# A transformer block on one core: a second score tile in some cycles goes to VectorE, and the opening of the attention loop is rearranged

## The chip, the core and the metric

One core of a Trainium2 chip. TensorE does the matmuls, ScalarE (ACT) the exponentials, VectorE (DVE) everything elementwise and a part of the exponentials, GpSimd (POOL) sets memory, and the queue of SyncE (SP) issues most of the DMAs. The metric is the device time of one execution in microseconds; it was measured three times before the change.

## What is computed

```python
h   = x + attention(layernorm(x)) @ wo      # S = 2048, D = 512, 32 heads of 16
out = h + (sigmoid(g) * u) @ w_down         # g, u = layernorm(h) @ w_gate, w_up; F = 1792
```

The attention is plain softmax over all 2048 keys. With 32 heads it needs 32 x 2048 x 2048 exponentials, which is most of the work of the kernel: the heads are so thin (16) that the matmuls around them are short.

## The kernel before, in words

**Prologue** (to 35.9 us). x is loaded, normalised and transposed into `xnT`; K and Q of the first block of eight heads and the first V tiles are computed; and a bound for the softmax is put in a spare row of `QB`, so that no maximum has to be taken later. The last thing before the loop is that bound: `q_bound` (L187) on VectorE writes `bnd`, and `emit_q_bound` (L216) sends two DMAs from it into `QB[0]`, one for heads 0 and 1 of the group, one for heads 2 and 3.

**Main loop** (35.9 to 936 us). The unit is a score tile: 128 keys by 512 queries of one head. Units run over query chunk `qc` (4), group of four heads `g` (8), key tile `kt` (16) and head `j` (4): 2048 units, in **steps** of three (`GU`), 683 steps in all. In a step, `emit_scores` (L669) has TensorE write three banks of `pss` (two such buffers, taken in turn) and ScalarE turn them into bf16 weights `pt` by one ACTIVATE over 1536 columns (L691). `emit_pv` (L739) multiplies four tiles at a time by V into `acc`. Four steps make a **cycle** (`CYC`): twelve units.

Three things set the pace of a cycle:

- In a *split* step the ACTIVATE takes two of the three tiles. The third goes to VectorE, which computes the exponential by bit operations and a polynomial, in five instructions: `exp_bits` in the step itself (L703; it reads `pss`), two of `exp_first` a step later (L706, L709), `exp_second` two steps later (L712) and `exp_third` three steps later (L716). From step `G0` = 28 on, the first step of each cycle is split, save for three in each of chunks 1 to 3, just after the chunk before has ended: 154 steps.
- *Pairs*: the keys of heads 0, 1 and of heads 2, 3 lie in different halves of the rows of the array. From step 28 on every second step uses matmuls of 64 rows (`tile_position`), so that two of different halves can run side by side; the others use all 128 rows.
- *PV batches*: from step 28 on the twelve PV matmuls of a cycle are issued together in the third step of the next cycle; before that, four at a time (`plan_pv`, L799).

**Fill.** Between the scores, `emit_fill` (L759) hands out other matmuls, so many to a step (`rate`, L664): the remaining V tiles, K and Q of the later heads (`fill_v`, `fill_k`, `fill_q0`), Q of the later chunks (`fill_q`), then for each finished chunk the output projection, the second layer norm and the gated feed-forward layer (`ffn_tasks`). All of these share **one** PSUM bank, `pm`: a fill task that needs it waits until VectorE (or ScalarE for the gate's tanh, L496) has read the previous one. A task yields `("gap", n)` where it wants n further steps of rest before the next. What is computed must be ready when a later step asks for it, and the instructions of each engine run in the order in which they were issued; this order is written out by hand (`manual_schedule`), so a wait on any engine holds all that is issued after it there.

**Normalisation.** After the last key tile of a head group, `emit_norm` (L719) copies `acc`, sends the four rows of sums through DRAM into a `[32, 64]` tile, takes reciprocals on VectorE five steps later (L730), sends them back as rows broadcast over partitions, and multiplies ten steps later into `OT` (L736). This happens 31 times.

**Tail** (936 to 991 us). The feed-forward layer of the last chunk, which can't start before the last head is done.

Of the kernel before, what the change touches and what calls it, by code (L numbers as in the profile page):

```python
# [9 lines left out]
FP32 = mybir.dt.float32  # L10
# [7 lines left out]
def kernel(  # L18
# [11 lines left out]
    nc = tc.nc  # L30
    P = 128
# [8 lines left out]
    QC = 512  # L40
    TQ = QC // P
    NQC = S // QC
    GU = 3
    CYC = 4
    RATES = ((2.0, 2.0, 0.0, 3.0), (2.0, 2.5, 0.0, 3.0))
    G0 = 28
    GM = 188
    G1 = 680
    QS = DH ** -0.5 * 1.4426950408889634 * 2.0 ** 23
# [9 lines left out]
    norm = ctx.enter_context(tc.tile_pool(name="norm", bufs=1))  # L59
# [18 lines left out]
    for part in (1, 0, 2):  # L78
        nc.scalar.dma_start(out=wqkv_sb[:, :, part * D:(part + 1) * D],
                            in_=wqkv_v[:, :, part * D:(part + 1) * D])  # L80
# [132 lines left out]
            nc.sync.dma_start(out=QB[n % 2][32 * j:32 * j + 32:2, j, :],  # L213
                              in_=QTu[r:r + DH, g // 2, qc * QC:(qc + 1) * QC])

    def emit_q_bound(n):  # L216
        qc, g = qgs[n]
        assert ("b", qc, g // 2) in ready
        r = 32 * qc + 4 * g
        for h in range(2):  # L220
            nc.sync.dma_start(out=QB[n % 2][64 * h + 1:64 * h + 2, 2 * h:2 * h + 2, :],
                              in_=bnd[r + 2 * h:r + 2 * h + 2, :])

    NV0 = 6
# [1 line left out]
    def prologue(pro):  # L226
# [137 lines left out]
        k_bound()  # L364
        q_bound(0, False)
        ready.add(("b", 0, 0))
        emit_q_bound(0)
        k_spread(ku, 1, slice(0, S), nc.sync)
        gate = pro.tile([32, 1], BF16, name="gate")
        nc.gpsimd.tensor_copy(out=gate[:], in_=bnd[0:32, 0:1])  # L370
# [5 lines left out]
    NS = len(groups)  # L376
    SPC = NS / NQC
# [17 lines left out]
    def fill_k(b):  # L395
        ku = stages[b % 2]
        sqs = []
        for n in range(5):
            if n < 4:
                ps = pm_tile()  # L400
                for c in range(DC):
                    yield 1
                    qk_mm(ps, 1, b, n, c)
                cols = slice(n * QC, (n + 1) * QC)
                nc.vector.tensor_copy(out=ku[:, cols], in_=ps[:])
                sqs.append(squares(ku[:, cols]))
                if n in (0, 2):
                    nc.gpsimd.memset(KT[:, 2 * b + n // 2, :], 1.0)
                yield ("gap", 0)
            if n:  # L410
                pn = pm_tile()
                yield 1
                norm_mm(pn, b, sqs[n - 1][:])
                k_max(pn, b, n - 1)
                yield ("gap", 0)
        for g in (2 * b, 2 * b + 1):
            k_spread(ku, g, slice(0, S), nc.sync)
        k_bound()
        ready.add(("k", b))
# [4 lines left out]
    def fill_q0(b):  # L424
        ps = pm_tile()
        for c in range(DC):
            yield 1
            qk_mm(ps, 0, b, 0, c)
        q_store(QTu[:, b, 0:QC], ps)
        sq = squares(QTu[:, b, 0:QC])  # L430
        yield ("gap", 2)
        pn = pm_tile()
        yield 1
        norm_mm(pn, b, sq[:])
        q_root(pn, 0)
        q_bound(0, True)
        ready.add(("q", 0, b))
        ready.add(("b", 0, b))
        yield ("gap", 0)

    def fill_q(qc):
        cols = slice(qc * QC, (qc + 1) * QC)
        sq4 = stages[qc % 2]
        for b in range(4):
            ps = pm_tile()
            for c in range(DC):
                yield 1
                qk_mm(ps, 0, b, qc, c)
            q_store(QTu[:, b, cols], ps)
            nc.vector.tensor_tensor(out=sq4[:, b * QC:(b + 1) * QC], in0=QTu[:, b, cols], in1=QTu[:, b, cols],  # L450
                                    op=ALU.mult)
            ready.add(("q", qc, b))
            yield ("gap", 3)
        yield ("gap", 2)
        pn = pm_tile()
        for b in range(4):
            yield 1
            norm_mm(pn, b, sq4[:, b * QC:(b + 1) * QC], start=(b == 0), stop=(b == 3))
        q_root(pn, qc)
        q_bound(qc, False)  # L460
        for b in range(4):
            ready.add(("b", qc, b))
        yield ("gap", 0)

    def wo_mm(ps, t, g):
        nc.tensor.matmul(ps[:], lhsT=OT[t // TQ % 2][:, g, t % TQ * P:(t % TQ + 1) * P], rhs=wo_pad[:, g, :],  # L466
# [195 lines left out]
        yield from wo_early(NQC - 1)  # L662

    def rate(i):  # L664
        if i < G0:
            return 4.0 if i < 6 else 2.0
        return (RATES[i >= 3 * SPC][(i - G0) % CYC], 1.0, 1.0, 0.0)[n_pv.get(i, 0)]

    def emit_scores(i):  # L669
        group = groups[i]  # L670
        n = len(group)
        pss = pss2[i % 2]
        pairs = i >= G0 and (i - G0) % 2 == 1
        order = list(enumerate(group))
        if pairs and group[0][3] // 2 == group[1][3] // 2:
            order[1:] = order[:0:-1]
        for ui, (qc, g, kt, j) in order:
            n_qg = qc * NG + g
            assert ("k", g // 2) in ready
            h0 = 64 * (j // 2)  # L680
            rows = slice(h0, h0 + 64) if pairs else slice(0, P)
            nc.tensor.matmul(pss[:, ui, :], lhsT=KT[rows, g, kt * P:(kt + 1) * P],  # L682
                             rhs=QB[n_qg % 2][rows, j, :], start=True, stop=True,
                             tile_position=(h0, 0) if pairs else None)
            if kt == 12 and j == 3 and n_qg + 1 < len(qgs):
                emit_q_rows(n_qg + 1)
                emit_q_bound(n_qg + 1)
        k = (i - G0) % 7 if i >= G0 else i % 4
        pt = pt4[k] if k < 4 else (pt_early if i < GM else pt_late)[k - 4]
        na = n - 1 if i in split else n  # L690
        ex = nc.scalar.activation(out=pt[:, 0:na, :], in_=pss[:, 0:na, :], func=ACT.Exp, scale=DH ** -0.5 / QS)  # L691
        if na < n:
            scratch = early_scratch if i < GM else late_scratch
            tc.declare_no_dep(exp_bits(pss[:, na, :], *scratch).ins, ex.ins,
                              reason="both only read, from different banks")
            later(i + 1, lambda: exp_first(*scratch))
            later(i + 2, lambda: exp_second(*scratch))
            later(i + 3, lambda: exp_third(pt[:, na, :], *scratch))
        for ui, u in enumerate(group):
            p_of[u] = pt[:, ui, :]  # L700

    def exp_bits(src, e_bits, e_man, e_pol):
        return nc.vector.tensor_scalar(out=e_bits, in0=src, scalar1=ONE_BITS, scalar2=0.0, op0=ALU.add, op1=ALU.max)  # L703
# [15 lines left out]
    def emit_norm(qc, g, i):  # L719
        xs = norm.tile([P, QC], FP32, name="xs")  # L720
        nc.vector.tensor_copy(out=xs[:], in_=acc[:])  # L721
        sd = dram.tile([4, QC], FP32, name="sd")
        for j in range(4):
            nc.sync.dma_start(out=sd[j:j + 1, :], in_=xs[32 * j + DH:32 * j + DH + 1, :])
        s32 = norm.tile([32, 64], FP32, name="s32")
        nc.sync.dma_start(out=s32[:], in_=sd[:].rearrange("j (a b) -> (j a) b", b=64))

        def recip():
            r32 = norm.tile([32, 64], FP32, name="r32")
            nc.vector.reciprocal(out=r32[:], in_=s32[:])  # L730
            rd = dram.tile([4, QC], FP32, name="rd")
            nc.sync.dma_start(out=rd[:].rearrange("j (a b) -> (j a) b", b=64), in_=r32[:])
            rb = norm.tile([P, QC], FP32, name="rb")
            for j in range(4):
                nc.sync.dma_start(out=rb[32 * j:32 * j + 32, :], in_=rd[j:j + 1, :].to_broadcast([32, QC]))
            later(i + 10, lambda: nc.vector.tensor_tensor(out=OT[qc % 2][:, g, :], in0=xs[:], in1=rb[:], op=ALU.mult))  # L736
        later(i + 5, recip)
# [52 lines left out]

    LAG = 2

    split = set(range(G0, G1, CYC))
    for qc in range(1, NQC):
        n0 = int(qc * SPC) + 20
        split -= {n for n in range(n0, n0 + 24) if (n - G0) % (2 * CYC) == 0}


    def plan_pv():  # L799
        plan, last = {}, 0  # L800
        for n, group in enumerate(groups):
            if G0 <= n < G1:
                if (n - G0) % CYC == 0:
                    last = n + CYC + 2
                    for k, u in enumerate(units[n * GU:(n + CYC) * GU:4]):
                        if k and u[2] == 0:
                            last += 1
                        plan.setdefault(last, []).append(u)
            else:
                for u in group:  # L810
                    if u[3] == 3:
                        last = max(last, n + LAG)
                        plan.setdefault(last, []).append(u)
        return plan

    with tc.manual_schedule():
# [13 lines left out]
        later(90, lambda: nc.gpsimd.tensor_copy(out=ident_f[:], in_=ident_bf[:]))  # L830
        load_w()
        pv_due = plan_pv()
        n_pv = {i: len(us) if G0 <= i < G1 + CYC else 0 for i, us in pv_due.items()}
        for i in range(NS + LAG):
            if i < NS:
                emit_scores(i)
            for fn in due.pop(i, []):
                fn()
            for u in pv_due.pop(i, []):
                emit_pv(*u[:3], i)  # L840
            if LAG <= i < NS:
                emit_fill(i)
        for _ in fl:
            pass
# [35 lines left out]
```

## Time and profile before

| | |
|---|---|
| median of three runs | 990.5 us (988.42 to 992.69) |
| the profiled execution's own time | 993.14 us, its span 991.4 us |
| main loop in it, first to last exponential | 35.9 to 936.0 us |
| granted TensorE clock, mean | 0.993 |
| an ACTIVATE of 3 tiles / of 2 tiles (128x1536, 128x1024) | 1.49 us / 1.08 us |
| the five VectorE instructions of a split tile | 0.69, 0.42, 0.69, 0.69, 0.68 us |

How to read it: the busy share of an engine (page, part 1) is a mean over a prologue, a long loop and a tail, which have different limits, so the loop is cut into stages by time, and in each stage the question is which engine the next step waited for. ACTIVATEs overlap: one of three tiles lasts 1.49 us, but the next one starts after 1.33 us. The time that counts is that from start to start.

### The profile page before, as it was taken

The numbers are of one execution on the slowest core, as the hardware profiler recorded it, in microseconds if no ns is written. First come the engines' busy times: TensorE is split into PE (matmuls) and PEld (weight loads), VectorE is DVE, ScalarE is ACT, GpSimd is POOL, SyncE is SP. The second block draws the span as 40 slices with busy tenths as digits, with TensorE's granted clock in tenths as the row PEclk, the third lists the DMA queues.
The fourth block names the chain that finished last, engine by engine and source line by source line (L and its number), as shares of the span: only waits on it lengthen the run. The fifth ranks groups of instructions, "written<-read, shape, count | busy, mean of one in ns | idle before, by whom it ended". The sixth has DMA issues, their size and how long they took to land.

```text
span 991.4 us, 14443 instructions
## 1 busy us (share of the span) xinstructions
PE 848.8 (86%) x5197; PEld 282.9 (29%) x5291; DVE 696.1 (70%) x1202; ACT 910.5 (92%) x772; POOL 41.3 (4%) x57
## 2 busy tenths in 40 slices
PE   4898888878788888989888888899888888889998
PEld 2332222222222222223222222223222222223343
DVE  8338898888775776767766777777766776767452
ACT  4799899999999999999999999999999999999731
POOL 4600000000000000000000000000000000000000
PEclk9999999999999999999999999999999999999999
DMA  5002331000003000000000000000100000000100
GB/s 156 20 1 54 101 82 54 15 16 4 20 20 100 15 15 16 14 6 28 26 21 26 16 15 15 15 2 26 32 25 21 15 15 15 14 6 22 45 1 21
DMA packets 26400, 28.06 MB, mean 28 GB/s; under 512 B 8348, under 2 KB 20764, under 8 KB 26328
## 3 DMA queue, kind: packets, MB, share of 16 engines
q1 hardware_dynamic: 24744, 25.56, 9.1%
q10 hardware_dynamic: 1584, 1.57, 0.5%
q8 instruction: 41, 0.67, 0.3%
q14 instruction: 31, 0.25, 0.1%
HBM read 20.18 MB, written 2.61 MB: 23 GB/s over the span
## 4 chain that ended last, share of the span: by engine, by line
PE 49%; ACT 30%; DVE 13%; issue 5%; DMA 1%; POOL 0%; SPq 0%; ACTq 0%; DVEq 0%; POOLq 0%
PE pss L682 24%; ACT pt L691 15%; PE acc L742 9%; ACT stg L691 7%; PE pm L504 5%; ACT QTu L691 4%; PE pm L487 3%; ACT wd L691 3%; PE pm L491 2%; PE pm L466 2%; PE pm L156 2%; ACT sg L496 2%; DVE wd L703 1%; PE pm L151 1%; DVE st L130 1%
## 5 line engine op out<-in xcount | busy, mean ns | idle before, releaser
L682 PE MATMUL pss<-QB,KT 64*128 64x512 bf16 (+1 forms) x2022 | 487.5, 381 | 92.4 <-ACT pt L691 44.3
L691 ACT ACTIVATE pt<-pss 128x1536 bf16<-128x1536 f32 (+1 forms) x404 | 527.3, 1402 | 13.2 <-PE pss L682 12.1
L682 PEld LDWEIGHTS <-KT 128*128 128x128 bf16 (+1 forms) x2048 | 152.4, 95 | 370.0 <-issue 257.4
L691 ACT ACTIVATE stg<-pss 128x1536 bf16<-128x1536 f32 (+1 forms) x140 | 185.9, 1393 | 4.8 <-PE pss L682 4.7
L703 DVE TENSOR_SCALAR stg<-pss 128x512 int32<-128x512 f32 x114 | 78.8, 691 | 129.7 <-PE pss L682 126.2
L742 PE MATMUL acc<-pt,Vaug 128*17 128x512 bf16 x1211 | 115.8, 384 | 2.3 <-DVE xs L721 1.7
L691 ACT ACTIVATE QTu<-pss 128x1024 bf16<-128x1024 f32 (+1 forms) x71 | 98.7, 1390 | 0.4 <-PE pss L682 0.2
L691 ACT ACTIVATE wd<-pss 128x1024 bf16<-128x1024 f32 (+1 forms) x68 | 88.0, 1373 | 2.4 <-PE pss L682 2.0
L709 DVE SCALAR_TENSOR_TENSOR y<-reg 128x512 f32<-128x512 f32 x114 | 79.0, 693 | 3.9
L712 DVE SCALAR_TENSOR_TENSOR y<-y,reg 128x512 f32<-128x512 f32 x114 | 78.6, 690 | 3.3
L487 PE MATMUL pm<-reg,reg 128*128 128x512 bf16 x212 | 62.1, 380 | 10.4 <-DVE reg L500 9.4
L742 PEld LDWEIGHTS <-Vaug 128*17 128x17 bf16 x2048 | 37.8, 89 | 110.3 <-issue 93.6
L491 PE MATMUL pm<-reg,wu 128*128 128x512 bf16 x206 | 62.5, 382 | 1.6 <-issue 1.3
L500 DVE SCALAR_TENSOR_TENSOR reg<-sg,pm 128x512 bf16<-128x512 f32 x56 | 38.3, 683 | 32.1 <-PE pm L491 28.9
L504 PE MATMUL pm<-wd,reg 128*128 128x512 bf16 x211 | 58.8, 381 | 2.0 <-issue 1.3
L742 PE MATMUL acc<-stg,Vaug 128*17 128x512 bf16 x420 | 49.7, 382 | 1.6 <-DVE xs L721 1.6
L706 DVE TENSOR_SCALAR reg<-stg 128x512 int32<-128x512 int32 x114 | 48.4, 424 | 2.8
L496 ACT ACTIVATE sg<-pm 128x512 f32<-128x512 f32 x56 | 35.0, 624 | 16.7 <-PE pm L487 15.6
L156 PE MATMUL pm<-reg 128*128 128x512 bf16 x115 | 35.9, 388 | 7.5 <-DVE y L167 3.7
L703 DVE TENSOR_SCALAR wd<-pss 128x512 int32<-128x512 f32 x40 | 27.5, 688 | 20.7 <-PE pss L682 20.3
L716 DVE SCALAR_TENSOR_TENSOR pt<-y,stg 128x512 bf16<-128x512 f32 x61 | 41.2, 675 | 1.2
L466 PE MATMUL pm<-wo_pad,OT 128*128 128x512 bf16 x117 | 34.9, 382 | 1.0 <-DVE reg L475 0.4
(108 smaller groups left out, 603.2 us busy)
## 6 DMA issues: line engine op xcount, KB each, us to landing
rb<-rd SPq DMA_DIRECT2D x124, 64.0 KB
reg<-in_A_x_dram SPq DMA_DIRECT2D x8, 256.0 KB
QB<-QTu SPq DMA_DIRECT2D x128, 16.0 KB
xr<-in_A_x_dram SPq DMA_DIRECT2D x16, 128.0 KB
out_dram<-ob SPq DMA_DIRECT2D x16, 128.0 KB
sd<-xs SPq DMA_DIRECT2D x124, 2.0 KB
KT<-stg SPq DMA_DIRECT2D x7, 256.0 KB
reg<-in_B_w_gate_dram SPq DMA_DIRECT2D x4, 448.0 KB
```

Of the source, the lines that this page charges most:

```text
L156: nc.tensor.matmul(ps[:], lhsT=wqkv_sb[:, c, w0:w0 + P], rhs=xnT[:, c, n * QC:(n + 1) * QC], start=(c == 0), stop=(c == DC - 1))
L466: nc.tensor.matmul(ps[:], lhsT=OT[t // TQ % 2][:, g, t % TQ * P:(t % TQ + 1) * P], rhs=wo_pad[:, g, :], start=(g == 0), stop=(g == NG - 1))
L487: nc.tensor.matmul(ps[:], lhsT=wg[:, c, f * P:(f + 1) * P], rhs=hnT[:, c, :], start=(c == 0), stop=(c == DC - 1))
L491: nc.tensor.matmul(ps[:], lhsT=wu[:, c, f * P:(f + 1) * P], rhs=hnT[:, c, :], start=(c == 0), stop=(c == DC - 1))
L496: nc.scalar.activation(out=sg[:], in_=ps[:], func=ACT.Tanh, scale=0.5)
L504: nc.tensor.matmul(ps[:], lhsT=hT[:, f, tt * P:(tt + 1) * P], rhs=wd[:, f, :], start=(f == 0), stop=(f == FC - 1))
L682: nc.tensor.matmul(pss[:, ui, :], lhsT=KT[rows, g, kt * P:(kt + 1) * P], rhs=QB[n_qg % 2][rows, j, :], start=True, stop=True, tile_positio ...
L691: ex = nc.scalar.activation(out=pt[:, 0:na, :], in_=pss[:, 0:na, :], func=ACT.Exp, scale=DH ** -0.5 / QS)
L703: return nc.vector.tensor_scalar(out=e_bits, in0=src, scalar1=ONE_BITS, scalar2=0.0, op0=ALU.add, op1=ALU.max)
L709: nc.vector.scalar_tensor_tensor(out=e_pol, in0=m, scalar=PA, in1=m, op0=ALU.add, op1=ALU.mult)
L712: nc.vector.scalar_tensor_tensor(out=e_pol, in0=e_pol, scalar=PB, in1=e_man.bitcast(FP32), op0=ALU.add, op1=ALU.mult)
L742: nc.tensor.matmul(acc[32 * j:32 * j + VW, :], lhsT=Vaug[:, kt, 4 * g + j, :], rhs=p_of.pop((qc, g, kt, j)), start=(kt == 0), stop=(kt == ...
```

## The change

- `split` begins at step 8 instead of 28, and a second split step is added in one of four cycles (`twice`): the third step of cycles that begin at a multiple of 16. That is 29 more, from step 114 to step 658, none of them in the first 45 steps of chunks 1 to 3. Together 188 split steps for 154. The second tile has scratch memory of its own, in the half of `OT` that isn't in use (`scratch_of`).
- PV batches of twelve and the ring of seven `pt` buffers run from step 0, and so does the alternation of pairs. Up to step 44, and in the cycles with two splits, every step uses pairs. 421 steps use them instead of 327.
- `rate`: to step 44, fill of 4, 4 (2 from step 12), 0 and 4 matmuls in the steps of a cycle; 2, 2, 0, 3 in cycles with two splits. Fill starts in step 1 rather than 2. `fill_k` for b > 1, the end of `fill_q0` and the end of `fill_q` each rest one more step.
- The sums are laid out as `[128, 16]` instead of `[32, 64]` for the reciprocal.
- The second of the two first DMAs of the bound is issued from ScalarE's queue instead of SP's.

```diff
-    G0 = 28
+    FIRST = 44
...
-    def emit_q_bound(n):
+    def emit_q_bound(n, engs=(nc.sync, nc.sync)):
...
-            nc.sync.dma_start(out=QB[n % 2][64 * h + 1:64 * h + 2, 2 * h:2 * h + 2, :],
+            engs[h].dma_start(out=QB[n % 2][64 * h + 1:64 * h + 2, 2 * h:2 * h + 2, :],
                               in_=bnd[r + 2 * h:r + 2 * h + 2, :])
...
-        emit_q_bound(0)
+        emit_q_bound(0, (nc.sync, nc.scalar))
...
                     nc.gpsimd.memset(KT[:, 2 * b + n // 2, :], 1.0)
-                yield ("gap", 0)
+                yield ("gap", int(b > 1))
...
                 k_max(pn, b, n - 1)
-                yield ("gap", 0)
+                yield ("gap", int(b > 1))
...
         ready.add(("q", 0, b))
         ready.add(("b", 0, b))
-        yield ("gap", 0)
+        yield ("gap", 1)
...
         for b in range(4):
             ready.add(("b", qc, b))
-        yield ("gap", 0)
+        yield ("gap", 1)
...
     def rate(i):
-        if i < G0:
-            return 4.0 if i < 6 else 2.0
-        return (RATES[i >= 3 * SPC][(i - G0) % CYC], 1.0, 1.0, 0.0)[n_pv.get(i, 0)]
+        if i < FIRST:
+            rates = (4.0, 4.0 if i < 12 else 2.0, 0.0, 4.0)
+        elif i - i % CYC + 2 in twice:
+            rates = (2.0, 2.0, 0.0, 3.0)
+        else:
+            rates = RATES[i >= 3 * SPC]
+        return (rates[i % CYC], 1.0, 1.0, 0.0)[n_pv.get(i, 0)]
...
-        pairs = i >= G0 and (i - G0) % 2 == 1
+        pairs = i % 2 == 1 or i < FIRST or i - i % CYC + 2 in twice
...
-        k = (i - G0) % 7 if i >= G0 else i % 4
+        k = i % 7
...
-            scratch = early_scratch if i < GM else late_scratch
+            scratch = scratch_of(i)
...
+    def scratch_of(i):
+        if i % CYC:
+            flat = OT[(int((i - 20) / SPC) + 1) % 2][:].rearrange("p g q -> p (g q)")
+            return (flat[:, 0:2 * QC].bitcast(mybir.dt.int32), flat[:, 2 * QC:4 * QC].bitcast(mybir.dt.int32),
+                    flat[:, 4 * QC:6 * QC].bitcast(FP32))
+        return early_scratch if i < GM else late_scratch
...
-        s32 = norm.tile([32, 64], FP32, name="s32")
-        nc.sync.dma_start(out=s32[:], in_=sd[:].rearrange("j (a b) -> (j a) b", b=64))
+        s32 = norm.tile([P, 16], FP32, name="s32")
+        nc.sync.dma_start(out=s32[:], in_=sd[:].rearrange("j (a b) -> (j a) b", b=16))
...
-    split = set(range(G0, G1, CYC))
-    for qc in range(1, NQC):
-        n0 = int(qc * SPC) + 20
-        split -= {n for n in range(n0, n0 + 24) if (n - G0) % (2 * CYC) == 0}
+    split = set(range(8, G1, CYC))
+    twice = set()
+    for qc in range(NQC):
+        n0 = int(qc * SPC) + 20
+        if qc:
+            split -= {n for n in range(n0, n0 + 24) if n % (2 * CYC) == 4}
+        lo, hi = (int(qc * SPC) + 45, int((qc + 1) * SPC) + 16) if qc else (112, int(SPC) + 16)
+        twice |= {n + 2 for n in range(lo, min(hi, G1 - 8)) if n % (4 * CYC) == 0}
+    split |= twice
...
-            if G0 <= n < G1:
-                if (n - G0) % CYC == 0:
+            if n < G1:
+                if n % CYC == 0:
...
-            if LAG <= i < NS:
+            if 1 <= i < NS:
                 emit_fill(i)
```

## The prediction, made before the changed kernel ran

> **What bounds the kernel now.** I read the page's busy shares first, since they say which engine to look at:
>
> ```profile
> PE 848.8 (86%) x5197; PEld 282.9 (29%) x5291; DVE 696.1 (70%) x1202; ACT 910.5 (92%) x772; POOL 41.3 (4%) x57
> ```
>
> ScalarE is busy 92% of a span that has a tail and a prologue without exponentials. So the second view is its timeline in the middle of the loop, for the time from start to start:
>
> ```profile
> 568.71 0.60 ACT L496 ACTIVATE sg<-pm 128x512 f32<-128x512 f32 x1
> 569.19 1.04 ACT L691 ACTIVATE stg<-pss 128x1024 bf16<-128x1024 f32 x1
> 570.09 1.49 ACT L691 ACTIVATE QTu<-pss 128x1536 bf16<-128x1536 f32 x1
> 571.42 5.10 ACT L691 ACTIVATE pt<-pss 128x1536 bf16<-128x1536 f32 x4
> 576.37 0.65 ACT L496 ACTIVATE sg<-pm 128x512 f32<-128x512 f32 x1
> ```
>
> Nothing stands between them: three tiles cost 1.33 us, two 0.92 (0.90 here, 0.94 in most cycles), a tanh 0.48. A split tile saves ScalarE 0.41. The loop has 529 ACTIVATEs of three tiles, 154 of two and 42 tanh: 706 + 142 + 20 = 869 us, and lasts 900. The other 31 us are waits of ScalarE. The third view, busy time by stretch (columns: length, then PE, PEld, DVE, ACT, POOL, then the clock), says where they are:
>
> ```profile
> 35.90:83.50 47.60, 44.31 (x239) 15.48 (x242) 18.65 (x34) 44.71 (x33) 12.63 (x9) 1.00 0.05 11
> 83.50:190.60 107.10, 88.39 (x547) 26.92 (x557) 95.07 (x169) 100.81 (x81) 0.00 (x0) 0.98 0.24 65
> 77.60:144.90 67.30, 56.21 (x334) 16.88 (x337) 62.13 (x118) 60.96 (x49) 0.00 (x0) 0.97 0.28 77
> 190.60:291.10 100.50, 81.40 (x519) 25.53 (x526) 79.50 (x134) 99.28 (x81) 1.07 (x2) 0.98 0.06 18
> 291.10:936.00 644.90, 564.07 (x3532) 180.66 (x3594) 453.16 (x746) 635.48 (x534) 9.53 (x22) 1.00 0.07 21
> ```
>
> These are steps 0 to 32, 32 to 112, 28 to 76 (inside the two), 112 to 192, and the rest. By the same count ScalarE needs 42.3, 98.6, 98.6 and 629.5 us in the four that tile the loop, so it waits 5.3, 8.5, 1.9 and 15.4. In the first TensorE is full (93%); in steps 28 to 76 VectorE is (92%), because fill and split tiles meet there. From 291 on ScalarE bounds, with single stalls of this kind (VectorE, TensorE, ScalarE):
>
> ```profile
> 589.70 0.69 DVE L703 TENSOR_SCALAR stg<-pss 128x512 int32<-128x512 f32 x1 [2.10 <-PE pss L682]
> 590.30 0.68 DVE L736 TENSOR_TENSOR OT<-xs,rb 128x512 bf16<-128x512 f32 x1
> 590.90 0.68 DVE L500 SCALAR_TENSOR_TENSOR reg<-sg,pm 128x512 bf16<-128x512 f32 x1
> ```
> ```profile
> 591.64 0.59 PE L487 MATMUL pm<-reg,reg 128*128 128x512 bf16 x2 [0.89 <-DVE reg L500]
> 592.07 0.81 PE L682 MATMUL pss<-QB,KT 128*128 128x512 bf16 x3
> ```
> ```profile
> 592.97 2.79 ACT L691 ACTIVATE pt<-pss 128x1536 bf16<-128x1536 f32 x2 [0.63 <-PE pss L682]
> ```
>
> The up product (L500) frees `pm`, but stands third in VectorE's queue; the fill matmul of the next step waits 0.89 for it, the scores stand behind that matmul, and ScalarE runs dry. This is the price of a crowded VectorE, and the change crowds it.
>
> **The change, part by part.**
>
> *The bound on two queues.* SP issues the two DMAs at 32.36 and 33.13; the second lands at 34.74 and the first scores start at 34.93. On ScalarE's queue the second stands behind the three V copies, the last of which runs from 34.25 to 34.84. An issue takes 0.60, and landing follows 1.0 after its end: 36.45, so the first exponential is **1.3 us** later. Bounds: 0 (the DMA isn't last after all) to 2.0.
>
> *Steps 0 to 32.* Matmuls are 0.216 apart. Scores as pairs take two slots for three, 0.43 for 0.65, and PV batches save changes between array shapes (gaps of 0.09). What decides is the single `pm` bank. A V tile of four matmuls takes 0.86, its copy starts 0.20 later (38.87 to 39.07) and lasts 0.69, and the next fill can start 0.06 after: 1.81 us where V tiles come in consecutive steps. Following the issue order (V in steps 1, 3, 4, 5, 7, 8, 9, 11, 12), steps 0 to 16 take 23.6 us (24.4 before). In steps 16 to 32 K chunks and their norms alternate in the same chain, 5.5 a cycle: 22.3 (23.2 before). Together **-1.7**, though ScalarE's need falls to 40.3: the six early split tiles buy little. Bounds: +1 to -5.
>
> *Steps 32 to 112.* From 28 to 76 VectorE's instructions, by the groups' durations in issue order, sum to 68.7 us and took 67.3, a ratio of 0.98. Afterwards fill has begun earlier and rests longer, and steps 8 to 108 hold 125 us of such work: 123 at that ratio, against 123.3 that ScalarE needs. So neither waits long for the other. I take ScalarE's 98.6 and 2 us for local crowding: 100.6 for 107.1, **-6.5**. Bounds: -8.5 to -2 (half of the waits stay as K's new pattern collides elsewhere).
>
> *Steps 112 to 192.* Five double cycles take ScalarE to 96.6; VectorE's sum is 101, 99 at the ratio. **-1.5**; bounds -3.9 to +1.
>
> *The rest.* 24 double cycles: 24 x 0.41 = 9.8 less for ScalarE. VectorE has 3.17 us more per double cycle: its mean here is 70%, and 24 x 3.17 = 76 us in 635 makes 82%, which fits. The queue in the moment does not. Count from the end of the second split's scores: bits, second, third, the two firsts, then the next cycle's bits, second, up product. With the pitches of the timeline (0.60 if independent, 0.72 and 0.45 in a chain) the up product ends at 4.9, or 5.5 where a normalisation stands in between (copy or `OT`). Where a feed-forward tile ends in the first step after a double cycle and a new one begins in the second, that fill matmul would like to start at about 3.6. By issue order this holds after eight of the 24 (224, 256, 288, 416, 448, 576, 608, 640), and in all eight a normalisation instruction is there too. I get 1.6 to 1.8 us of stall each, against 0 to 1.4, on average 0.5, in these cycles before: 8 x 1.2 = 9.6; two more (484, 656) pay about 1 at the down projection. The other cycles: the second tile's `exp_third` ends at 5.0, and TensorE reaches the third quarter of the PV batch, which needs it, at 5.1. No stall. Sum -9.8 + 9.6 + 2.0 = **+1.6**. Bounds: -9.8 (pairs in double cycles give TensorE 0.43 and all is absorbed) to +20.
>
> *At nothing.* The reciprocal of 64 elements takes 534 ns, of 1 element 164; of 16 by interpolation 250: 31 x 0.28 = 9 us of VectorE, in its free time. The 64-byte rows could land later; VectorE waits 1.9 us in all for `rb` now, so up to 0.5 x 31 the other way if the reciprocal comes to wait; I take 0. Scratch in `OT` falls in steps in which that half is unread. After the last step both orders have the same 599 instructions, so the tail stays.
>
> Sum: 1.3 - 1.7 - 6.5 - 1.5 + 1.6 = **-6.8**: the profiled 993.1 would be 986.3. The profiled execution is 2.6 above the median, so against that **983.7**.
>
> **The clock.** In three stretches the granted clock halves for 3.41 us, and the cycles there (56, 160, 352) are 2.5, 1.4 and 1.3 longer than ScalarE's need. The last one, with the stretch ahead of it:
>
> ```profile
> 497.30:500.70 3.40, 1.97 (x10) 0.64 (x9) 1.99 (x5) 3.40 (x4) 0.00 (x0) 1.00 0.12 41
> 500.70:504.10 3.40, 3.40 (x18) 0.60 (x17) 1.85 (x3) 2.69 (x2) 0.00 (x0) 0.50 0.26 58
> ```
>
> TensorE wasn't idle before it, only thinly used (some matmul records may be missing). The Trainium skill, "TensorE: Matmul & The Clock Gate", section "What's actually happening", lets the clock fall after an idle window of about 3.4 us; by that rule pairs could not cost clock, and these three falls should not be there. The length agrees, the condition does not: the trace shows no gap of TensorE near 3.4 us ahead of them. So I go by the row.
>
> **Rivals.**
>
> *All absorbed.* The stalls in the eight cycles stay at their old size, as TensorE, with pairs, is ahead: the rest gives -9.8, sum -18: 972. For: idle VectorE, 30% in the mean. Against: the queue above. 0.22.
>
> *The early gain doesn't come.* K's chain on `pm` holds steps 32 to 112 as now: -6.8 + 5.5: 989. For: one bank. Against: fill now comes every second step, so that its copy has time. 0.12.
>
> *The clock.* Cycles without fill issue 2.37 us of matmuls in 4.52 instead of 2.80 in 4.95. If the threshold lies there, seven more falls of 1.4 make 993.5. For: all falls came in thin stretches. Against: most stretches as thin had none. 0.08.
>
> *Slower.* VectorE stalls the scores after every late double cycle, not only eight: `exp_bits` holds the bank until it runs, and at 1.2 us a cycle 24 x 1.2 = 29 replaces the 11.6, so 983.7 + 17.4 = 1001. It decides against the change from about 0.8 a cycle. For: three tiles of 3.17, 9.5 us, fall in two cycles of 9.45. Against: bits ends at 3.7, the bank is wanted at 3.9. 0.10.
>
> **How the numbers follow.** The forecast, 983.7, has 0.48, with its own range 978 to 989 from the bounds of the small terms. The range that leaves out the slower end and a part of the best case is 971 to 994. A measurement here tells 0.5%, 985.5 to 995.5, from no change. Faster: 0.33 of the forecast, 0.22 of the absorbed case, 0.55 together. Same: 0.15 + 0.12 + 0.07 and a little of the slower case, 0.35. Slower: 0.10.
>
> **What would show it.** The first exponential at 37.2 instead of 35.9; steps 32 to 112 in about 100.6 with VectorE above 90%; 2-tile ACTIVATEs of 0.92 in the third step of double cycles; and in cycles 228, 292, 420, 612 the fill matmul waiting 1.5 us or more for the up product. I'd be wrong if those waits are as short as now, if the early steps don't shorten, or if the clock falls more than six times.

## The result, and the profile after

The changed kernel takes 1002.0 us in the median (999.42 to 1003.92 in four executions), the kernel before 990.9 us in the same session; the ratio is 1.0112 with an interval of 1.0080 to 1.0144. So it became slower, by about 11 us, and the forecast of 983.7 us and its range (to 994) were both missed. The profiled execution took 1002.22 us, with a span of 1000.4.

The page of the changed kernel: ScalarE has less work, as meant, VectorE has 84 us more, and the span is longer by 9.

```profile
PE 851.2 (85%) x5291; PEld 269.0 (27%) x5291; DVE 780.2 (78%) x1372; ACT 898.9 (90%) x772; POOL 41.5 (4%) x57
```

The busy time by stretch, in the same columns as before (length, then PE, PEld, DVE, ACT, POOL, clock): steps 0 to 32, 32 to 112, 112 to 192, 192 to 352, and 352 to the end of the loop.

```profile
34.90:80.70 45.80, 39.88 (x244) 10.84 (x242) 33.01 (x59) 41.94 (x33) 13.52 (x9) 1.00 0.07 17
80.70:181.30 100.60, 83.90 (x540) 24.43 (x540) 90.90 (x162) 99.55 (x80) 0.00 (x0) 1.00 0.25 67
181.30:285.40 104.10, 84.61 (x540) 24.90 (x539) 94.35 (x163) 98.51 (x82) 0.00 (x0) 0.98 0.07 17
285.40:502.30 216.90, 187.47 (x1168) 57.02 (x1169) 168.47 (x287) 205.22 (x175) 3.61 (x8) 0.98 0.09 25
502.30:945.10 442.80, 385.64 (x2430) 118.06 (x2430) 343.71 (x582) 423.57 (x360) 7.17 (x16) 0.99 0.07 18
```

The early stages became as short as forecast. Everything from step 112 on became longer, although ScalarE has less to do there. Stage by stage (us, from the first exponential of one step to that of the next):

| stage | forecast difference | before | after | difference |
|---|---|---|---|---|
| first exponential at | +1.3 | 35.9 | 34.9 | -1.0 |
| steps 0 to 32 | -1.7 | 47.6 | 45.7 | -1.9 |
| steps 32 to 112 | -6.5 | 107.2 | 100.7 | -6.5 |
| steps 112 to 192 | -1.5 | 100.4 | 104.1 | +3.7 |
| steps 192 to 352 | | 208.4 | 216.9 | +8.5 |
| steps 352 to 528 | | 231.1 | 233.8 | +2.7 |
| steps 528 to the end of the loop | | 205.4 | 209.0 | +3.6 |
| 192 to the end together | +1.6 | 644.9 | 659.7 | +14.8 |

The tail is unchanged, 55.3 us in both. The table's sum, +9.1, is that of the two profiled executions, of which the one of before lay 2.3 us above the 990.9. The first row is mostly the clock: in the profile of before it fell to half for 3.4 us at 29.7 us, in the prologue. Two later profiles with the old way of sending the bound and without that fall have their first exponential at 35.16, so the second queue is worth about 0.25 there.

What a cycle that became longer looks like is best read where the prediction had looked, at the feed-forward tile of the cycle that begins at step 420, right after a cycle with two split tiles. VectorE, from the second tile's `exp_bits` on, with TensorE's fill and ScalarE (left out after the first line are four more polynomial steps, which keep VectorE busy until 591.07):

```profile
587.99 0.69 DVE L714 TENSOR_SCALAR OT<-pss 128x512 int32<-128x512 f32 x1 [0.21 <-PE pss L686]
...
591.04 0.38 PE L491 MATMUL pm<-reg,wu 128*128 128x512 bf16 x1
591.24 0.69 DVE L714 TENSOR_SCALAR stg<-pss 128x512 int32<-128x512 f32 x1 [0.17 <-PE pss L686]
591.85 0.68 DVE L747 TENSOR_TENSOR OT<-xs,rb 128x512 bf16<-128x512 f32 x1
592.45 0.68 DVE L723 SCALAR_TENSOR_TENSOR OT<-OT 128x512 f32<-128x512 f32 x1
593.05 0.68 DVE L500 SCALAR_TENSOR_TENSOR reg<-sg,pm 128x512 bf16<-128x512 f32 x1
593.79 0.59 PE L487 MATMUL pm<-reg,reg 128*128 128x512 bf16 x2 [1.72 <-DVE reg L500]
594.22 0.81 PE L686 MATMUL pss<-QB,KT 128*128 128x512 bf16 x3
595.12 2.79 ACT L695 ACTIVATE pt<-pss 128x1536 bf16<-128x1536 f32 x2 [1.46 <-PE pss L686]
```

The up product's matmul is done at 591.42, but its reader on VectorE (L500) starts only at 593.05: `exp_bits` of the new cycle, the normalisation and `exp_second` of the second tile (the one whose tiles are named `OT`) stand ahead of it. It frees `pm` at 593.73, 5.74 after the second tile's `exp_bits` began (the prediction counted 5.5). The next fill matmul waits 1.72 us for it, the scores stand behind that matmul, and ScalarE is idle for 1.46 us. A second tile saves ScalarE 0.41.

The waits of the changed kernel by stretch show that this is the common case from step 192 on, and another one between 112 and 192 (columns: who <- whom, us in total, times, longest). First steps 112 to 192, where the profile shows no wait of TensorE for `pm`, but the scores wait for `exp_bits` (L714) to free their bank, and PV for the weights that `exp_third` (L727) writes:

```profile
ACT pt L695 <- PE pss L686: 3.8, 5, 1.6
PE pss L686 <- DVE wd L714: 3.6, 5, 1.1
PE acc L753 <- DVE wd L727: 1.5, 2, 0.9
```

Then steps 192 to the end:

```profile
PE pm L487 <- DVE reg L500: 17.1, 17, 1.7
ACT pt L695 <- PE pss L686: 16.1, 16, 2.7
...
PE pm L504 <- DVE ob L509: 4.0, 6, 1.3
...
PE pm L504 <- DVE reg L500: 2.4, 2, 1.5
PE pss L686 <- DVE stg L714: 2.4, 6, 0.6
```

Here the waits for the one fill bank `pm` come to 23.5 us (17.1 + 4.0 + 2.4), those for the score bank to 2.4.

The clock also falls more often inside the loop: five times, each time in the cycle that follows one with two split tiles. One of them, with the stretch ahead of it:

```profile
374.90:378.30 3.40, 1.58 (x8) 0.59 (x7) 3.37 (x7) 3.15 (x3) 0.00 (x0) 1.00 0.04 7
378.30:381.70 3.40, 3.40 (x20) 0.70 (x17) 2.64 (x6) 1.45 (x1) 0.00 (x0) 0.50 0.02 2
```

In the 3.4 us ahead VectorE is busy for 3.37 and TensorE for 1.58: TensorE is waiting for VectorE. Then it runs at half speed for 3.4 us, and is the bound for that time.

### The profile page after: what moved, and what is told of

Same layout as the page of the kernel before. It is cut to its first block, busy times and chain, and to the rows that moved or that the text cites. A ratio compares the mean times of both kernels' runs of the same rounds, so it can differ in the third digit from the quotient of the medians.

```text
span 1000.4 us, 14694 instructions
## 1 busy us (share of the span) xinstructions
PE 851.2 (85%) x5291; PEld 269.0 (27%) x5291; DVE 780.2 (78%) x1372; ACT 898.9 (90%) x772; POOL 41.5 (4%) x57
## 3 DMA queue, kind: packets, MB, share of 16 engines
q10 hardware_dynamic: 1588, 1.58, 0.5%
## 4 chain that ended last, share of the span: by engine, by line
PE 44%; DVE 25%; ACT 23%; issue 5%; DMA 2%; POOL 0%; SPq 0%; DVEq 0%; ACTq 0%; POOLq 0%
PE pss L686 21%; ACT pt L695 12%; PE acc L753 7%; PE pm L504 5%; ACT stg L695 4%; PE pm L487 4%; ACT QTu L695 3%; PE pm L491 2%; ACT wd L695 2%; PE pm L466 2%; DVE wd L714 2%; DVE pt L727 2%; DVE reg L500 1%; DVE y L723 1%; DVE wd L720 1%
## 5 line engine op out<-in xcount | busy, mean ns | idle before, releaser
L686 PE MATMUL pss<-QB,KT 64*128 64x512 bf16 (+1 forms) x2048 | 471.4, 383 | 89.4 <-ACT pt L695 42.4
L695 ACT ACTIVATE pt<-pss 128x1536 bf16<-128x1536 f32 (+1 forms) x392 | 502.2, 1365 | 26.7 <-PE pss L686 24.4
L686 PEld LDWEIGHTS <-KT 64*128 64x128 bf16 (+1 forms) x2048 | 137.2, 95 | 367.2 <-issue 262.5
L695 ACT ACTIVATE stg<-pss 128x1536 bf16<-128x1536 f32 (+1 forms) x140 | 181.8, 1354 | 8.8 <-PE pss L686 7.9
L714 DVE TENSOR_SCALAR stg<-pss 128x512 int32<-128x512 f32 x114 | 78.6, 690 | 80.3 <-PE pss L686 79.9
L695 ACT ACTIVATE wd<-pss 128x1024 bf16<-128x1024 f32 (+1 forms) x80 | 103.3, 1362 | 3.6 <-PE pss L686 2.2
L695 ACT ACTIVATE QTu<-pss 128x1024 bf16<-128x1024 f32 (+1 forms) x71 | 96.1, 1354 | 4.1 <-PE pss L686 3.8
L487 PE MATMUL pm<-reg,reg 128*128 128x512 bf16 x224 | 64.9, 381 | 17.5 <-DVE reg L500 17.1
L504 PE MATMUL pm<-wd,reg 128*128 128x512 bf16 x224 | 61.7, 385 | 6.5 <-DVE ob L509 4.0
L491 PE MATMUL pm<-reg,wu 128*128 128x512 bf16 x224 | 66.4, 382 | 0.0
L500 DVE SCALAR_TENSOR_TENSOR reg<-sg,pm 128x512 bf16<-128x512 f32 x56 | 38.3, 684 | 27.3 <-PE pm L491 27.3
L727 DVE SCALAR_TENSOR_TENSOR pt<-y,stg 128x512 bf16<-128x512 f32 x61 | 41.5, 680 | 1.2
L714 DVE TENSOR_SCALAR wd<-pss 128x512 int32<-128x512 f32 x45 | 30.9, 686 | 9.4 <-PE pss L686 7.6
```

What stands on the lines that cost most here:

```text
L487: nc.tensor.matmul(ps[:], lhsT=wg[:, c, f * P:(f + 1) * P], rhs=hnT[:, c, :], start=(c == 0), stop=(c == DC - 1))
L491: nc.tensor.matmul(ps[:], lhsT=wu[:, c, f * P:(f + 1) * P], rhs=hnT[:, c, :], start=(c == 0), stop=(c == DC - 1))
L500: nc.vector.scalar_tensor_tensor(out=hT[:, f, :], in0=sg[:], scalar=1.0, in1=ps[:], op0=ALU.add, op1=ALU.mult)
L504: nc.tensor.matmul(ps[:], lhsT=hT[:, f, tt * P:(tt + 1) * P], rhs=wd[:, f, :], start=(f == 0), stop=(f == FC - 1))
L727: nc.vector.scalar_tensor_tensor(out=dst, in0=e_pol, scalar=PC, in1=e_bits.bitcast(FP32), op0=ALU.add, op1=ALU.mult)
```

## The experiments

The theory after the result: *the queue of VectorE*. After a second tile, work that frees a bank for TensorE stands behind polynomial steps, so a double cycle (one with two split tiles) is paid back with more than its 0.41 in the cycle that follows, and the clock falls come from these stalls. The rivals: the falls are the cause and come from the *pairs* in the double cycles (the prediction's clock rival); or the early rearrangement and the *rests* cost as much as the tiles. Ratios below are against the kernel before on the same chip in the same session, with their intervals; its medians in the four sessions, 990.0 to 990.9, are close enough to compare microseconds across them. Stages are those of one profiled execution each.

**The second tiles taken out of the change** (the one edit in the changed kernel):

```diff
-    split |= twice
+    twice = set()
```

> The changed kernel without any second split tile; all else of the change stays. Queue theory (the second tile crowds VectorE's queue in the moment, and that costs more than the 0.41 us it saves ScalarE) and clock theory (pairs in the double cycles thin out TensorE, and its clock falls) both say about 981: the kernel before less 9.3 us gained by step 112. If the early gain is lost again later, or the opening causes the loss, it stays near 1000. From step 192 on the loop should take 645 us, as in the kernel before.

988.14 us, ratio 0.9979 (0.9964 to 0.9993): 13.9 us below the changed kernel. From step 112 on, with columns as above (steps 112 to 192 and 192 to 352):

```profile
181.50:280.70 99.20, 83.55 (x540) 26.49 (x539) 80.99 (x138) 99.04 (x81) 0.00 (x0) 1.00 0.07 18
280.70:493.00 212.30, 186.21 (x1168) 59.15 (x1169) 146.48 (x247) 207.89 (x176) 3.60 (x8) 1.00 0.09 26
```

The 104.1 and 216.9 of the changed kernel are 99.2 and 212.3 here, its 442.8 to the end of the loop are 435.2, with ScalarE busy longer and no clock fall in the loop. Cycle by cycle, in excess of what ScalarE needs: from step 112 on the changed kernel has 29.1 us more than this one (whose profiled execution, 985.3 us, is 2.8 below its median), and 23.6 of them, clock falls included, lie in the 29 cycles that directly follow a cycle with two splits, 1.8 in the double cycles themselves. That places the loss. It isn't in all 29: 15 of the cycles that follow lose more than 0.41, and 10 less than 0.1. But 212.3 for steps 192 to 352 is still 3.9 above the kernel before (208.4), without a single second tile: a second loss, with another cause.

**The second tiles alone, put into the kernel before** (with their scratch, their pairs and their `rate`):

```diff
+    twice = set()
+    for qc in range(NQC):
...
+        twice |= {n + 2 for n in range(lo, min(hi, G1 - 8)) if n % (4 * CYC) == 0}
+    split |= twice
```

> The kernel before with the 29 second split tiles alone (their scratch, pairs and rate with them), with the old opening and gaps. Queue and clock theory: the kernel before plus 14 to 20 us, 1005 to 1011. If the loss needs the new opening (fill that is left over later), about 991.

1006.09 us, ratio 1.0169 (1.0142 to 1.0196), +16.1: they cost as much without the rest of the change. There are six clock falls in the loop, the first of them before the first second tile. The early part isn't needed for the loss.

**No added pairs** (changed kernel; double cycles alternate like the others):

```diff
-        pairs = i % 2 == 1 or i < FIRST or i - i % CYC + 2 in twice
+        pairs = i % 2 == 1 or i < FIRST
```

> The changed kernel, but the double cycles keep full-row matmuls in their first and third step. Queue theory: 1000 to 1004, the same, as VectorE's work is the same. Clock theory: the falls of the clock in the loop go from 5 to 3 or fewer, 993 to 998.

1007.06 us, ratio 1.0160 (1.0122 to 1.0197), no better than the changed kernel, with five falls in the loop, one of them twice as long. The falls don't come from the pairs; that rival is out. Nor are the falls the main part of the loss: one of the four executions, at a mean clock of 0.997, still took 999.8 us, where the kernel without second tiles takes 986.2 to 987.6 at 0.996 to 0.998.

**A light second tile** (changed kernel; the second tile gets only `exp_bits` and `exp_third`, so the polynomial steps of 29 tiles are left out; ScalarE's work stays as in the change):

```diff
+            if i in twice:
+                later(i + 3, lambda: exp_third(pt[:, na, :], scratch[0], scratch[1], scratch[0].bitcast(FP32)))
+            else:
...
```

> The changed kernel, but the second split tile gets two VectorE instructions instead of five: the exponential of 29 tiles is left out (first and second polynomial step), so these weights are wrong. ScalarE still saves 0.41 us a tile and TensorE's pairs stay. Queue theory: the stalls go, 970 to 976. Clock theory: the falls stay, 992 or more.

976.60 us, ratio 0.9879 (0.9850 to 0.9908): 25.4 below the changed kernel, and 11.5 below the one without second tiles, which is 29 x 0.41 = 11.9 to within the intervals. So relieving ScalarE does pay in full, as long as VectorE isn't crowded: against the kernel without second tiles, the three instructions left out decide between -11.5 and +13.9. VectorE is still busy for 88% of steps 112 to 192 (86.5 of 97.9 us) and 74% of the rest (474.2 of 640.1); the changed kernel has 91% and 78%. A mean over a stage would not have told the two apart.

**The order alone** (changed kernel; all five instructions stay, but in the five steps from a second split on the fill, with VectorE's reads of `pm`, is issued ahead of the due polynomial steps and PV):

```diff
+            crowded = any(n in twice for n in range(i - 4, i + 1))
+            if crowded and 1 <= i < NS:
+                emit_fill(i)
             for fn in due.pop(i, []):
...
-            if 1 <= i < NS:
+            if not crowded and 1 <= i < NS:
                 emit_fill(i)
```

> The changed kernel; in the third step of a double cycle and the four steps after it, the fill is issued ahead of the polynomial steps that are due, so that what frees the fill's bank stands ahead of them in VectorE's queue. VectorE's work is the same. If the stalls come through the single fill bank: the eight stalls of 1.6 shrink to 0.5 or less and falls of the clock go with them, 990 to 995. If they come through the score banks or the PV batch: 1000 to 1004.

988.82 us, ratio 0.9985 (0.9971 to 0.9998): 13.2 below the changed kernel with the same work on every engine. The same cycle as above in this kernel:

```profile
584.91 0.69 DVE L714 TENSOR_SCALAR stg<-pss 128x512 int32<-128x512 f32 x1 [0.17 <-PE pss L686]
...
585.51 0.68 DVE L500 SCALAR_TENSOR_TENSOR reg<-sg,pm 128x512 bf16<-128x512 f32 x1
...
586.11 0.69 DVE L747 TENSOR_TENSOR OT<-xs,rb 128x512 bf16<-128x512 f32 x1
586.25 0.59 PE L487 MATMUL pm<-reg,reg 128*128 128x512 bf16 x2 [0.52 <-DVE reg L500]
...
587.58 1.45 ACT L695 ACTIVATE pt<-pss 128x1536 bf16<-128x1536 f32 x1 [0.25 <-PE pss L686]
```

The up product stands second instead of fourth in VectorE's queue from the new cycle's `exp_bits` on; the fill waits 0.52 instead of 1.72, ScalarE 0.25 instead of 1.46. From step 192 on the waits for `pm` come to 14.3 us instead of 23.5. In this profile the only fall of the clock in the loop begins at 35.2 us, in its first step; the other nine executions have mean clocks of 0.990 to 0.998, so in some of them it does. The issue order and `pm` are thus a cause that is shown. Two limits: the edit also puts the fill ahead of PV on TensorE, and the two were not tried apart; and 13.2 us is only half of the 25.4 between the changed kernel and the light second tile. Of the 10.4 us that the profiles of the light tile and of this kernel still differ by, 5.7 lie in steps 112 to 192, which stay long (103.5 us): there it isn't `pm` that is waited for, and VectorE is busy for 94.6 of them.

**The rests.** The second loss. `fill_q` and `fill_k` rest one more step in the change. The kernel without second tiles, with the old rests:

```diff
-                yield ("gap", int(b > 1))
+                yield ("gap", 0)
...
-        yield ("gap", 1)
+        yield ("gap", 0)
```

> No second split tile, and the three longer rests undone (gaps of 0 as before); the new opening alone. The first feed-forward part then begins at step 185 as in the kernel before, not at 188. If the place of the feed-forward part against the cycles matters: 983 to 986, steps 192 to 352 in 208.5. If the rests are what gave the gain of steps 32 to 112: that stage goes from 100.9 to 104 or more and the time is 988 or above.

988.78 us, ratio 0.9990 (0.9973 to 1.0006), the same as with the new rests, but by two opposite effects: steps 32 to 112 take 106.3 instead of 100.9 (the rests in `fill_k` and `fill_q0` are worth 5.4 there), steps 192 to 352 take 208.8 instead of 212.2. What the rests move there is the start of the first feed-forward part: the last rest of `fill_q` puts off the first output projection from step 184 to step 187. The first tanh of the tiles then come at steps 224, 231, 237, 244, 251 instead of 223, 229, 235, 241, 247. So, again without second tiles, I shortened the rests inside `fill_q` of the last chunk, keeping the others, to start this part as early as in the kernel before:

```diff
-            yield ("gap", 3)
-        yield ("gap", 2)
+            yield ("gap", 3 if qc < 3 else 2)
+        yield ("gap", 2 if qc < 3 else 1)
```

> No second split tile, longer rests kept, but Q of the last chunk rests one step less after each part, so that the first feed-forward part begins at step 185. Place theory: steps 192 to 352 in 208.5 instead of 212.2, 984. If not: 988, as with no second split tile alone.

982.74 us, ratio 0.9922 (0.9905 to 0.9940), 7.2 below the kernel before. Steps 192 to 352 are back at the old length, 208.4 us.

And the converse, the kernel before with that part begun three steps late:

```diff
-            yield ("from", int((qc + 1) * SPC) + 15)
+            yield ("from", int((qc + 1) * SPC) + (15 if qc else 18))
```

> The kernel before, with the first feed-forward part told to begin three steps later, at step 188 (where the changed kernel begins it). Place theory: 3.8 us slower, 994, with steps 192 to 352 in 212. If the place doesn't matter: 990.

993.40 us, ratio 1.0030 (1.0016 to 1.0044); steps 192 to 352 take 211.3 instead of 208.4. The delay costs 2.9 there by itself. At the old start the first tiles need six steps each, at the new one now six and now seven, so I read it as a matter of phase against the cycles; a third start was not tried.

One of the delayed waits goes through SyncE's queue. In the changed kernel, before the first scores of chunk 2 (step 341), its issues and the wait of TensorE are:

```profile
471.13 9.27 SPq L511 DMA_DIRECT2D out_dram<-ob  x2
480.50 3.85 SPq L213 DMA_DIRECT2D QB<-QTu  x4
484.41 1.26 SPq L221 DMA_DIRECT2D QB<-bnd  x2
486.09 0.60 PE L686 MATMUL pss<-QB,KT 64*128 64x512 bf16 x2 [1.44 <-DMA QB<-bnd]
```

and in the kernel with the earlier part:

```profile
464.46 0.36 SPq L511 DMA_DIRECT2D out_dram<-ob  x1
...
467.38 1.26 SPq L221 DMA_DIRECT2D QB<-bnd  x2
```

The output row block that comes ahead of Q's rows in SyncE's queue waits in the changed kernel for the down projection (L509, 479.34 to 480.02), and Q's bound behind it is issued 17 us later than with the earlier part. Some 7 of these are the lag of the whole loop; the other 10 are the queue's: the issue comes 6.8 us after the start of step 335 here, 3.3 ahead of it there. The scores wait for the bound for 1.44 us, and a clock fall follows.

**What could be had.** Three combinations. Fill first in all steps from 44 on, on top of the earlier feed-forward part and so without second tiles:

```diff
+            if 44 <= i < NS:
+                emit_fill(i)
...
-            if 1 <= i < NS:
+            if 1 <= i < 44:
```

> As e7_ffn_at_185 (no second split tile), with the fill issued ahead of the polynomial steps and normalisations that are due in every step from 44 on. Queue theory: the stalls of 0.8 to 1.3 us of the kernel before, where a normalisation stands ahead of the up product, shrink by 0.6 each: 979 to 981. If delaying the polynomial steps costs as much in the PV batch: 983 to 986.

986.73 us, ratio 0.9960 (0.9947 to 0.9973), 4 above the kernel that it started from (982.74): steps 32 to 112 take 108.0 instead of 100.9, one clock fall among it, and the three feed-forward stages gain 3.8 (1.5, 1.3 and 1.0). As a rule for all steps the order is worse. In steps 32 to 112 VectorE then waits 8.9 us for the fill's matmuls, whose readers stand ahead in its queue (1.9 with the old order), and the scores 9.4 us for `exp_bits`, which shares that queue, to free their bank (2.2).

The better order and the earlier feed-forward part together, with all second tiles (the edits of the two experiments):

> As e5_fill_first (all 29 second tiles, fill ahead of what is due in the crowded steps), with the first feed-forward part at step 185. If place and queue order add up: 988.8 less 3.5 to 5.5, 983 to 985.5, no better than e7_ffn_at_185 without second tiles: second tiles are then worth nothing here. If the second tiles were worth their 0.41 us each once the order is right: 972 to 976.

992.13 us, ratio 1.0012 (1.0001 to 1.0023): a clear miss. The two gains don't add. In its profile steps 112 to 192 take 108.9 us (103.5 with the better order alone) with two falls of the clock, the first of them twice as long as usual, and two more falls follow at 500.9 and 716.0 us. The shorter rests move Q's matmuls into other steps of that stage; that VectorE has no room there is my reading, which no run tests. The stage between 192 and 352 did shorten, to 209.2.

Second tiles only where no stall had followed them, five in all, as an edit of the kernel with the earlier feed-forward part:

```diff
-    twice = set()
+    twice &= {354, 434, 514, 562, 626}
+    split |= twice
```

> As e7_ffn_at_185, with a second split tile in five cycles alone, those after which no fill matmul of the next step waits for VectorE (steps 354, 434, 514, 562, 626). Queue theory: each keeps its 0.41 us, 980 to 981.5. If any second tile costs by its mere work on VectorE: 983 to 986.

981.58 us, ratio 0.9913 (0.9895 to 0.9931). It is the fastest median of the kernels that leave nothing out, 1.2 below the same kernel without second tiles (982.74); the intervals overlap, and 5 x 0.41 = 2.1 is all that could be hoped for. This version and the one without second tiles beat both kernels.

## Why the prediction was wrong

The step that failed is **"The rest"**: forecast +1.6 (its three terms, -9.8 + 9.6 + 2.0, add up to +1.8), measured +14.8. It had the mechanism, work on VectorE that stands ahead of a reader of `pm`, but took all that it didn't name for nothing. Its terms, from the cycles of the two profiles:

| term of the rest | forecast | measured |
|---|---|---|
| ScalarE's work, 24 x 0.41 | -9.8 | -9.9 |
| the eight cycles after 224, 256, 288, 416, 448, 576, 608, 640 | +9.6 | +13.0 |
| the two others that were named (cycle 484, and 660, the one after 656) | +2.0 | +2.6 |
| the cycle after 336 | 0 | +3.3 |
| the other 13 cycles that follow a double one | 0 | +1.0 |
| everything else in these steps | 0 | +4.8 |

- *The eight stalls* were found and sized rightly: in the five without a clock fall ScalarE's need is exceeded by 1.56, 1.56, 1.56, 1.65 and 1.77, where 1.6 to 1.8 had been forecast, and the four named fill waits are there (1.72 in the one shown). The other three also had a fall of the clock and exceed it by 2.9 to 3.3. A fall adds about 1.35 us, three of them 4.0; without them the term is 9.0 for 9.6.
- *"The other cycles ... No stall"* holds for 13 of them, which lose 1.0 together, and not for the one after 336: 3.3, by the wait for Q's rows shown above, which begins without second tiles (1.05 there), grows with them, and has a clock fall on top.
- *The shift of the first feed-forward part* was left out: 2.9 in the kernel before with that part begun late, 3.8 from the kernel with the earlier part. In the kernel without second tiles 1.9 of these 3.8 lie in "everything else", 1.0 in the cycle after 336 and 0.8 in the one after 224. The prediction had the new tanh steps in its issue order (its 224, 256, 288 follow from it), but priced only the stalls after double cycles, neither the lost phase of the cycles in between nor what queues behind a later output store.
- *VectorE's mean* was to rise from 70% to 82% (its own figures give 83) with 24 x 3.17 = 76 us. Its busy time rose by 59 us, to 78%, because its instructions overlap (0.69 us long, 0.60 from start to start). The mean decides nothing here.
- *Steps 112 to 192*: -1.5 forecast, +3.7 measured. This is the second step that failed. The bound by VectorE's sum was 99; but its work isn't spread evenly. Around step 132 it ran without a pause for 9.7 us (203.96 to 213.61), with the fill of Q, a normalisation and the split tiles, and TensorE and the clock fell behind. The light second tile, with 86.5 us of VectorE's busy time instead of 94.4, took 97.9: the stage turns between these two.
- *The clock* was a rival of its own, with a cause in the pairs, at 0.08. The number of falls in the loop did rise, from three to five, but full rows gave five as well, and the profile with the better order only the one at the start. In the changed kernel each follows a stall: a surcharge on the main mechanism, not a rival to it.

The *slower* rival came nearest, with 1001 us, but that is luck. It priced a stall of 1.2 us after every late double cycle; the comparison with the kernel without second tiles gives 0.76 in the mean of the 24, falls included, and 13 of them lose only 0.1 each in the mean. The shift and steps 112 to 192 make up the difference. Its mechanism is the smaller part: after step 192 the score bank held by `exp_bits` makes 2.4 us of waits, `pm` 23.5 (against 11.9 without second tiles). Only in steps 112 to 192, which it did not speak of, is the score bank what is waited for.

What was right:

- *Steps 0 to 32*, -1.9 for -1.7, and *32 to 112*, -6.5 for -6.5, with VectorE at 90%. Of the second, a part is luck: the profile of before had a clock fall in that stage. In the experiment that begins the feed-forward part of the kernel before later, and is that kernel up to step 184, the stage takes 105.7 without a fall. So the edits are worth about 5 and the fall about 1.5. Freed of second tiles and of the shift, this early part gives 7.2 in the medians (forecast, with the start: 1.3 - 1.7 - 6.5 = -6.9).
- *The bound on ScalarE's queue* depends on the clock in the prologue. Where it falls there, as in the profile of before, the third V copy is late, the issue behind it too, and the scores can start at 36.45; the first exponential is at 37.2. That is so in the experiment with the earlier feed-forward part. The forecast has both to the digit, but by luck: the issue began at 34.34, while the copy (to 34.84) still ran; it took 1.41 instead of 0.60, and the scores started 0.70 after its end instead of 1.0; the errors cancel. In the profiled execution of the change it didn't fall, and the V copies were early:

```profile
32.58 0.59 ACT L203 CAST Vaug<-pm 128x512 bf16<-128x512 f32 x1 [0.28 <-PE pm L151]
32.66 1.16 ACTq L221 DMA_DIRECT2D QB<-bnd  x1
```

- *The reciprocal* of 16 elements takes 245 ns (250 forecast), and VectorE waits 5.2 us for `rb` instead of 1.9, in the kernel without second tiles 5.0; it does not decide anything here.

What stays open: when exactly the clock falls (the last section narrows it to where a stall lies, not to a sharp limit); what of the second tiles' cost in steps 112 to 192 would go with another order; and why the two gains of the last but one experiment collide.

## What to carry to other kernels

Work moved to an engine that is idle 30% of the time is paid for in its queue, not in its mean: for each place look at what stands behind the moved instructions, above all a reader that frees a bank for the bound engine. Where the work has to go there, try the issue order first, and only where the waits show it: here the same instructions cost 13 us more or less by what they stand in front of, and the same order in all steps was worse. And a rest of one step in an early stage can shift the start of a stage far behind it, so that a change of several parts is to be tried part by part.

## What the runs showed of the hardware

- The granted clock falls to half for about 3.4 us without a gap of TensorE anywhere near that length: in the 7 us ahead of the five falls in the loop its longest gap is 1.65 us. In the kernel before it is 0.6 ahead of two of the three, and a gap of 1.22 us lies around the start of the other (118.4). Executions of one kernel differ by the falls: without second tiles 985.2 us at a mean clock of 1.000, 990.7 at 0.991.
- In each profile the falls lie on one grid of 3.413 us: those of the kernel before, at 118.42, 251.54 and 500.71, are 39 and 73 times 3.413 apart. I divided the loops of all 13 profiles along their grids. Each of the 30 falls follows a stretch in which TensorE was busy for at most 2.04 of the 3.41 us, and no fall follows any of the 3305 stretches with more (those within a fall left out). Of the 15 below 1.70, 14 were followed by a fall; of the 47 from 1.70 to 2.04, 16. So it matters how a stall lies on the grid: in the changed kernel the gap from 376.44 to 377.94 lies inside one stretch (busy for 1.59), and the clock falls; the longer one from 592.06 to 593.79 is shared between two (2.13 and 2.94), and it doesn't. Busy time of TensorE is modelled, and some records may be missing, so the limit isn't sharper than this.
- A DMA on ScalarE's queue is issued while the instruction ahead of it still runs: the copy ran from 32.58 to 33.17, and the issue began at 32.66. It took 1.16 us there (1.41 in the profile with the earlier feed-forward part), where one on SyncE's queue took 0.70.
